# Whole-batch mixer sums in four column groups, more crossbar transposes and two-chunk exps in a fused attention and mixer kernel

## The chip, the cores and the metric

The kernel runs on one core of one Trainium2 chip. A core has five engines with queues of their own: TensorE (PE, matmuls; PEld is its weight load), VectorE (DVE), ScalarE (ACT), GpSimd (POOL) and SyncE (SP, which here only issues DMAs). Matmul results go to PSUM, eight banks of 128 partitions by 512 fp32. The metric is the device time of one execution in microseconds. The kernel before takes 286.63 us (median of 8 runs, 285.79 to 287.54).

## What is computed

Block-sparse attention over 4 batches, 8 heads, 768 positions and 64 channels a head, followed by a mixer. Blocks are 32 positions; the allowed blocks are the band, the first and last block, and three drawn blocks for each block of queries.

```python
scores = np.matmul(q, k.transpose(0, 1, 3, 2)) / np.sqrt(D)
scores = np.where(mask, scores, -1000000000.0)
attn = np.exp(scores - np.max(scores, axis=-1, keepdims=True))
attn = attn / (np.sum(attn, axis=-1, keepdims=True) + 1e-09)
x = np.matmul(attn, v)                  # (4, 8, 768, 64), then to (4, 768, 512)
h = x.transpose(0, 2, 1) @ U @ V        # U (768, 32), V (32, 768)
u = x + h.transpose(0, 2, 1)
out = u + np.maximum(u @ w_ch1, 0.0) @ w_ch2    # 512 -> 2048 -> 512
```

## The kernel before, in words

**Pairs and chunks.** Two heads make a pair; pair i belongs to batch i // 4, so there are 16 pairs. Keys are cut into six chunks g of 128. Scores are kept transposed: keys on partitions, 768 queries along the row. For each pair q, k and v are loaded in fp32 by SP (load_qk, load_v, two buffers each), cast to fp16 by POOL (cast, L132), and queries and keys are turned so that channels lie on partitions.

**Batch 0 and the later batches differ.** In batch 0 the mask is part of the contraction: qres and kres hold 64 channels of one head and 24 rows of a block bias. Each score step (S, L662) is two matmuls of 384 columns into two banks and one exp over one chunk of 768 on ACT (e). In the later batches the scores of both heads run as two row groups of 64 partitions (half_quad, L681, called by Q for both heads and by H for one); each head's exp covers two chunks (1536), and DVE multiplies the result by a 0/1 mask tile (p, L707). That mask tile is made in batch 0 (K and k). Exps land in est, 16 chunk slots handed out in twos (take_est).

**Turning.** Pairs 1 to 5 are turned on PE (turn_qk, R, six transposes for q and six for k) and copied by DVE (t). From pair 6 on, front (L371) does it by two DMA transposes through the crossbar, issued on SP; they are called in loads (L714), which also issues the loads of pair i + 2 and starts the weight loads: w1 (four 512 KB casts issued by POOL) behind the casts of pairs 2 and 3, w2 behind those of pairs 5 and 6. In later batches loads is called behind a pair's mixer sums.

**Values and mixer.** A value step multiplies a chunk of est with v and a column of ones (L398; A for one chunk, V for all six chunks of a head), and DVE divides (v: a reciprocal and two multiplications, into xh in fp16 and xf in fp32). The mixer runs pair by pair. M (mix, L482) is six matmuls of U's chunk, padded with zeros to 128 columns, with xh; m copies the 128x128 result to a16. D (add, L510) multiplies by V, and d adds the result to xh (into u16) and to xf. The second d of a pair also has SP issue the DMA transpose of u16 into uT (L528). Pairs 2 and 3 of batch 0 instead form uT on PE (X, Y, copy y), with E and g for xf; the very last pair is turned on PE (T, L551, copy x).

**Channel layers.** U (w1, L569) is four matmuls of 384 columns, one for each uT of the batch, followed by a relu on ACT (a) or DVE (b). In the first six such steps, P does three of the four matmuls and C the last. W (w2, L593) is four of the 16 matmuls of one output tile; behind the last of them DVE adds xf (f) and SP sends the tile out. L is half a tile at the very end.

**The order** is written out by hand in PLAN: a word in capitals issues a PE step (its digit is the first PSUM bank), a small letter issues the oldest result of its kind on DVE or ACT. PE, DVE, ACT and SP run exactly in this order; POOL's order is left to the framework. The head of the order is, with the first exps, casts and value steps:

```python
PLAN = """
S0 S3 e Z7 e z S0 S5 e Z2 e A7 z S3 A A e S0 S5 e A R2 e S3 t R1 e A A t S5 v e S3 S1 e K6
...
"""
```

The start (L238 to L326) brings the first head of pair 0 in: one cast on DVE and one on ACT, then the keys' first half is turned before the queries.

Of the kernel before, what the change touches and what calls it, by code (L numbers as in the profile page):

```python
# [2 lines left out]

# [14 lines left out]
P = 128  # L18
# [3 lines left out]
def kernel(  # L22
# [109 lines left out]
    def cast(i, dst, ld):  # L132

        if i < NPE:
            return nc.gpsimd.tensor_copy(out=dst, in_=ld)
        for h in range(2):
            for ts in (slice(0, T // 2), slice(T // 2, T)):
                last = nc.gpsimd.tensor_copy(out=dst[:, h, ts], in_=ld[:, h, ts])  # L138
        return last
# [25 lines left out]
    NPE = HP + 2  # L165
# [64 lines left out]
    with tc.manual_schedule(  # L230
# [71 lines left out]
        first_cast(0, 0, nc.vector.tensor_copy)  # L302
        first_cast(0, 1, nc.scalar.copy)
        first_turn(1, 0)
        first_row(1, 0, nc.scalar.copy)
        mask_half(0)
        for c in range(2):
            first_turn(0, c)
            first_row(0, c, nc.scalar.copy)
        mask_row(0, 0, nc.vector.tensor_copy)  # L310
        first_turn(1, 1)
# [68 lines left out]
    slots_of = {}  # L380

    def take_est(i, h, j):

        n = free_est.pop(0)
        for u in range(2):
            slots_of[i, h, 2 * j + u] = n + u
        return n

    def drop_est(i, h, g):
        n = slots_of.pop((i, h, g))  # L390
        if g % 2:
            free_est.append(n - 1)
# [14 lines left out]
    class Batch:  # L407
        def __init__(self):
            self.xf = xpool.tile([P, T, HD], FP32, tag="xf", name="xf", bufs=2)
            self.a16 = misc.tile([P, HD], FP16, tag="a16", name="a16", bufs=2)  # L410
            self.uT = [
                upool.tile([P, S], FP16, tag=f"uT{cc}", name=f"uT{cc}")
                for cc in range(NCC)
            ]
# [6 lines left out]
    S0 S3 e Z7 e z S0 S5 e Z2 e A7 z S3 A A e S0 S5 e A R2 e S3 t R1 e A A t S5 v e S3 S1 e K6  # L421
    A0 e A k K5 S3 k A e S6 S1 e K5 A e A k A S3 v K6 R7 e k S1 t e S3 S5 e R0 e S1 t A7 A e S3
    A A e S5 K0 K2 e A k A k S3 v A0 A e S1 A S5 e A K7 e S3 k K1 R2 e k A S5 t R7 e S3 t A S1 e
    v M6 e K5 S3 m k A7 A e S1 A A e S3 D0 A e S5 d R2 e S3 t A S0 e v M6 e D2 m S3 d A5 A e S0
    K7 A e S3 k A K6 e S0 k A A e S3 v R2 e S6 t S0 e S3 e A5 A e A D7 A K6 d S1 k D0 A e S3 d
    M7 e S1 m X6 A e S3 v Y A7 e S0 y E2 A e S3 g X5 Y e E6 A y A g A A Q v R6 e e t M7 X6 m Y p
    H y R7 e p H t U6 e p H b U7 e p H b P6 p e E2 V7 g p C Q v a V6 e e U7 v p P0 a M1 C P2 m p
    a C U6 a D7 Q a d D6 e e d U7 b U6 p U0 b U7 p a E6 Q a g U7 e e U6 b P7 b p X2 C V0 a p V4
    v P5 v Y P7 y C C M0 a a W6 m D7 Q d W e e D7 W d p W U7 f p Q a U7 e e W6 b U7 p U0 b W p a
    Q W e e W p U2 f V7 a p Q v V6 e e U7 v p U0 a U2 b U6 p a M7 a Q m D7 e e W6 d W p D7 W d p  # L430
    Q W e e W7 f p U0 V6 b p V1 v U2 v U0 a U4 a M5 a U6 m D0 U1 a d D6 W a d Q U6 e e W b W p
    W6 f p Q W e e U7 W p a W p Q f U7 e e W6 b U7 p W b p Q W e e W p U0 f V7 a p Q v V6 e e U7
    v p U0 a M1 a U6 m p U4 a D3 U1 a d D7 U6 a d Q b U7 e e U6 b U7 b p U1 a V6 p a V0 v U7 v
    U4 a M3 a U7 m U6 b D4 U2 a d U7 a D6 Q a d U7 e e W6 b U7 p W a p Q U7 e e W b W p U7 f p Q
    a U7 e e W6 b U7 p U0 b U1 p b V7 a Q v W e e V7 p U0 v W a p Q M7 e e W m W7 f p D0 D6 W d
    d p W Q W e e W6 f p W V7 p V1 v U4 v U7 a M0 a U2 m D1 W a d D5 W d W7 f Q W e e W p W W6 f
# [402 lines left out]
```

## Time and profile before

| what | value |
|---|---|
| median of 8 runs | 286.63 us |
| the profiled execution's own time | 286.92 us |
| its span on the core | 284.9 us |
| granted clock | 1.00 |
| PE, DVE, ACT, POOL busy | 277.2, 197.0, 179.1, 69.8 us |
| first exp of a score, first two-head score set | 7.38, 44.34 us |
| DVE busy in 44.3 to 64.0 us | 19.10 of 19.70 us |

Busy time of PE is modelled and includes the overlap of pipelined matmuls, so PE's pace is read from the chain of work that ended last, where pieces follow each other without overlap. The chain's pieces are "start, length, what, how many instructions". The lists in order of time give start, length, engine, line, operation, names and, in brackets, the idle time before and what ended it. ACT's two-chunk exp takes 1449 ns, the one-chunk exp 814 ns, but they overlap a little when they follow each other.

### The profile page before, as it was taken

The numbers are of one execution on the slowest core, as the hardware profiler recorded it, in microseconds if no ns is written. First come the engines' busy times: TensorE is split into PE (matmuls) and PEld (weight loads), VectorE is DVE, ScalarE is ACT, GpSimd is POOL, SyncE is SP. The second block draws the span as 40 slices with busy tenths as digits, with TensorE's granted clock in tenths as the row PEclk, the third lists the DMA queues.
The fourth block names the chain that finished last, engine by engine and source line by source line (L and its number), as shares of the span: only waits on it lengthen the run. The fifth ranks groups of instructions, "written<-read, shape, count | busy, mean of one in ns | idle before, by whom it ended". The sixth has DMA issues, their size and how long they took to land.

```text
span 284.9 us, 6730 instructions
## 1 busy us (share of the span) xinstructions
PE 277.2 (97%) x2770; PEld 163.5 (57%) x2770; DVE 197.0 (69%) x360; ACT 179.1 (63%) x213; POOL 69.8 (24%) x160
## 2 busy tenths in 40 slices
PE   7879999999999999999999999999999999999995
PEld 3557775657456654567556564565745565555553
DVE  5777989998768966788687885666866888231121
ACT  4979998885668466675776627777588730424200
POOL 5376127703151053401351033500310000000000
PEclk9999999999999999999999999999999999999999
DMA  5799999978370588108460499303741103001012
GB/s 175 232 317 245 230 213 222 182 122 202 63 236 28 90 242 243 62 19 223 101 211 2 98 224 216 134 17 60 225 86 39 39 37 86 18 0 40 37 55 92
DMA packets 46466, 36.78 MB, mean 129 GB/s; under 512 B 28036, under 2 KB 42948, under 8 KB 46436
## 3 DMA queue, kind: packets, MB, share of 16 engines
q1 hardware_dynamic: 43280, 31.80, 41.2%
q0 software_dynamic: 2688, 4.19, 8.3%
q8 instruction: 21, 0.34, 0.5%
q10 hardware_dynamic: 468, 0.36, 0.4%
q14 instruction: 9, 0.07, 0.1%
HBM read 27.66 MB, written 6.29 MB: 119 GB/s over the span
## 4 chain that ended last, share of the span: by engine, by line
PE 87%; DVE 6%; DMA 2%; POOL 2%; issue 1%; ACT 1%; SPq 1%; DVEq 0%; POOLq 0%; ACTq 0%
PE ps L569 29%; PE ps L593 28%; PE ps L398 11%; PE ps L692 9%; PE ps L669 3%; DMA kld<-in_k_dram 2%; PE ps L482 2%; PE ps L516 2%; PE ps L613 1%; PE ps L644 1%; DVE xh L463 1%; ACT est L678 1%; DVE est L707 1%; DVE u L523 1%; DVE xf L463 1%
## 5 line engine op out<-in xcount | busy, mean ns | idle before, releaser
L701 ACT ACTIVATE est<-ps 128x1536 f16<-128x1536 f32 x72 | 100.4, 1449 | 31.3 <-PE ps L692 31.3
L569 PE MATMUL ps<-uT,w1t 128*128 128x384 f16 x512 | 95.6, 326 | 0.4 <-DVE xf L526 0.2
L593 PE MATMUL ps<-w2t,tT 128*128 128x512 f16 x368 | 88.8, 379 | 0.0
L707 DVE TENSOR_TENSOR est<-est,mask 128x1536 f16<-128x1536 f16 x72 | 69.0, 960 | 13.4 <-ACT est L701 13.2
L581 ACT ACTIVATE tT<-ps 128x384 f16<-128x384 f32 x87 | 42.2, 493 | 54.0 <-PE ps L569 52.5
L569 PEld LDWEIGHTS <-w1t 128*128 128x128 f16 x512 | 47.4, 98 | 36.9 <-issue 6.6
L593 PEld LDWEIGHTS <-tT 128*128 128x128 f16 x368 | 34.4, 98 | 36.5 <-issue 2.9
L398 PEld LDWEIGHTS <-est 128*128 128x128 f16 x1152 | 40.7, 97 | 7.0 <-issue 1.2
L583 DVE TENSOR_SCALAR tT<-ps 128x384 f16<-128x384 f32 x41 | 22.8, 555 | 30.8 <-PE ps L569 30.3
L138 POOL CAST stqld<-qld 128x192 f16<-128x192 f32 x40 | 16.3, 450 | 112.0 <-DMA qld<-in_q_dram 98.5
L398 PE MATMUL ps<-vt,est 128*128 128x65 f16 x1152 | 43.3, 193 | 0.1
L678 ACT ACTIVATE est<-ps 128x768 f16<-128x768 f32 x48 | 34.8, 814 | 2.4 <-PE ps L669 2.3
L692 PE MATMUL ps<-qpl,kpl 64*128 64x512 f16 (+1 forms) x288 | 31.3, 325 | 0.0
L669 PE MATMUL ps<-qres,kres 128*128 128x384 f16 x96 | 22.2, 324 | 0.9 <-DVE kres L654 0.5
L601 DVE TENSOR_TENSOR of<-xf,ps 128x512 f32<-128x512 f32 x23 | 15.8, 685 | 9.8 <-PE ps L593 9.6
L692 PEld LDWEIGHTS <-kpl 64*128 64x128 f16 x288 | 11.7, 94 | 15.4 <-issue 9.5
L523 DVE TENSOR_TENSOR u<-xh,ps 128x384 f16<-128x384 f16 x28 | 15.4, 552 | 6.9 <-PE ps L516 6.1
L463 DVE TENSOR_TENSOR xh<-ps,rcp 128x384 f16<-128x384 f32 x32 | 17.8, 558 | 1.1
L463 DVE TENSOR_TENSOR xf<-ps,rcp 128x384 f32<-128x384 f32 x32 | 17.5, 547 | 0.0
L138 POOL CAST stkld<-kld 128x192 f16<-128x192 f32 x40 | 15.5, 428 | 1.3 <-DMA kld<-in_k_dram 0.6
L138 POOL CAST vt<-vld 128x192 f16<-128x192 f32 x40 | 15.2, 420 | 1.7 <-PE ps L692 1.4
L526 DVE TENSOR_TENSOR xf<-xf,ps 128x384 f32<-128x384 f32 x28 | 15.3, 548 | 0.0
(81 smaller groups left out, 143.0 us busy)
## 6 DMA issues: line engine op xcount, KB each, us to landing
vld<-in_v_dram SPq DMA_DIRECT2D x16, 384.0 KB, 4.6
out_dram<-of SPq DMA_DIRECT2D x23, 256.0 KB, 2.1
qld<-in_q_dram SPq DMA_DIRECT2D x15, 384.0 KB, 4.4
kld<-in_k_dram SPq DMA_DIRECT2D x15, 384.0 KB, 6.8
w1t<-in_moe_w_ch_dram POOLq DMA_DIRECT2D x4, 512.0 KB, 10.6
w2t<-in_moe_w_ch_dram POOLq DMA_DIRECT2D x4, 512.0 KB, 6.9
qld<-in_q_dram SPq DMA_DIRECT2D x2, 192.0 KB, 2.5
uT<-u SPq DMA_TRANSPOSE x13, 2.8
```

Source lines behind the costliest of these rows:

```text
L138: last = nc.gpsimd.tensor_copy(out=dst[:, h, ts], in_=ld[:, h, ts])
L398: nc.tensor.matmul(pav[:, sc, :], est[:, n, sc * P : (sc + 1) * P], vts[b % 2][:, 2 * hp + h, g, 0 : D + 1], start=(g == 0 and sc == 0), s ...
L463: self.last = nc.vector.tensor_tensor(out=dst, in0=pav[:, :, 0:D], in1=rcp[:, :, None].broadcast_to([P, T, D]), op=ALU.mult,)
L569: nc.tensor.matmul(pt, w1t[:, cc, jj * P : (jj + 1) * P], bts[b].uT[cc][:, c * HS : (c + 1) * HS], start=(cc == 0), stop=(cc == NCC - 1), ...
L581: nc.scalar.activation(out=dst, in_=pt, func=AF.Relu)
L583: nc.vector.tensor_scalar_max(out=dst, in0=pt, scalar1=0.0)
L593: nc.tensor.matmul(po, tts[b, c, jj][:, s * P : (s + 1) * P], w2t[:, jj, :], start=(jj == 0), stop=(jj == NJJ - 1),)
L669: nc.tensor.matmul(ps[:, c], kT[:, h, g * P : (g + 1) * P], qT[:, h, c * HS : (c + 1) * HS], start=True, stop=True,)
L678: lambda: nc.scalar.activation(out=dst, in_=ps, func=AF.Exp, scale=0.125),
L692: nc.tensor.matmul(units[h][:, u * S + lo : u * S + hi], kT[drows[h], g * P : (g + 1) * P], qT[drows[h], lo:hi], start=True, stop=True, sk ...
L701: nc.scalar.activation(out=both[h], in_=units[h].rearrange("p (g n) -> p g n", g=2), func=AF.Exp, scale=0.125,)
L707: lambda: nc.vector.tensor_mul(out=both[h], in0=both[h], in1=mask[:, 2 * j : 2 * j + 2, :]),
```

## The change

- **Whole-batch mixer sum.** In batches 1 to 3 the four M steps become one, mix_all. It keeps only U's 32 real columns as weights and writes four groups of 32 partitions of one bank: group c takes some of the six position chunks, so the four groups together hold U's sum in four parts. V is copied by DMA into all four groups of 32 rows (at pair 6), so that D adds the parts up. The sum comes behind the batch's last division, and all eight D of the batch behind it.
- **In place.** D's result goes back into xh (six buffers instead of three); u16 is gone.
- **Crossbar.** Pair 2 is handled like pairs 0 and 1 (D and the DMA transpose instead of X, Y, E), and so is the last pair (T is gone). Pairs 4 and 5 are turned by front, at the beginning of pairs 2 and 4, instead of R.
- **Two-chunk exps.** B does chunks 0 and 1, or 3 and 4, of a head in batch 0 into three banks with one exp of 1536. Ten of these replace twenty S. The est slots of a head are taken as (0,1), (2,5), (3,4).
- **Start.** Both first casts are on DVE; the queries are turned and copied before the keys.
- **Loads.** In the later batches loads is called behind a pair's second division. All of w1 starts behind the casts of pair 4; w2 starts when pair 2's second d is done (hold: four one-element copies on POOL that read xh and write into w2t).
- **Order.** PLAN is a new order of 867 words instead of 921.

```diff
-        first_cast(0, 0, nc.vector.tensor_copy)
-        first_cast(0, 1, nc.scalar.copy)
-        first_turn(1, 0)
-        first_row(1, 0, nc.scalar.copy)
-        mask_half(0)
+        for n in range(2):
+            first_cast(0, n, nc.vector.tensor_copy)
         for c in range(2):
             first_turn(0, c)
             first_row(0, c, nc.scalar.copy)
+        mask_half(0)
         mask_row(0, 0, nc.vector.tensor_copy)
+        first_turn(1, 0)
+        first_row(1, 0, nc.scalar.copy)
         first_turn(1, 1)
...
     PLAN = """
-    S0 S3 e Z7 e z S0 S5 e Z2 e A7 z S3 A A e S0 S5 e A R2 e S3 t R1 e A A t S5 v e S3 S1 e K6
...
+    B3 e S6 B0 e Z5 e S3 z Z7 e A6 z B0 A A e R7 S3 t A A e R5 B0 t K7 S3 e k K5 e A k A7 v A B0
+    K5 A e S3 k A A e K5 A k v B0 K6 S3 e k R5 e A7 A t M6 S1 m K0 e S5 k A S3 e S1 e R0 e A A t
+    S5 A S3 e v e B0 D6 A5 e A d A K7 A S3 k A K6 e A k B0 v S3 e e B5 A2 K0 e A R1 k A S3 t A
...
         def divide(self, h, pav):
...
+            if h and self.i >= HP:
+                loads(self.i + 1)
...
             def sums():
-                nc.vector.tensor_add(
-                    out=self.u16[:, ts, :], in0=self.xh[:, ts, :], in1=pu
-                )
+                nc.vector.tensor_add(out=xh, in0=xh, in1=pu)
                 nc.vector.tensor_add(out=xf, in0=xf, in1=pu)
-                if c == 1 and self.i < NPAIR - 1:
+                if c == 1:
                     nc.sync.dma_start_transpose(
...
-                    if self.i >= HP:
-                        loads(self.i + 1)
+                    if self.i == XP - 1:
+                        hold(self.xh)
...
+    def mix_all(b, n):
+
+        bt = bts[b]
+        pa = bank(n, [P, HD], FP32)
+        tiles = [[(c, hp) for hp in range(HP)] for c in range(4)]
+        for c in range(4):
+            tiles[c] += [(4 + c // 2, 2 * (c % 2) + u) for u in range(2)]
+        for m in range(HP + 2):
+            for c in range(4):
+                sc, hp = tiles[c][m]
                 nc.tensor.matmul(
+                    pa[c * R : (c + 1) * R, hp * P : (hp + 1) * P],
+                    Ut[:, sc, 0:R], bt.xh[hp][:, sc, :],
+                    start=(m == 0), stop=(m >= HP), skip_group_check=True,
+                )
+        then("m", lambda: nc.vector.tensor_copy(out=bt.a16, in_=pa))
...
+    def two_scores(i, h, g, n):
+        ps = PS[:, n : n + 3, :].rearrange("p b n -> p (b n)")
+        qT, kT = augs[i]
+        s = take_est(i, h, g, g + 1)
+        for u, lo, hi in SPANS:
+            nc.tensor.matmul(
+                ps[:, u * S + lo : u * S + hi],
+                kT[:, h, (g + u) * P : (g + u + 1) * P],
+                qT[:, h, lo:hi],
+                start=True, stop=True, skip_group_check=True,
+            )
...
     def loads(i):
         behind = ExitStack()
-        if NPE <= i + 1 < NPAIR:
+        if HP + 1 < i + 1 < NPAIR:
             behind.enter_context(tc.issue_after(front(i + 1).ins))
...
-            with tc.issue_after(last.ins):
-                if i == 0:
-                    load_w1((0, 1))
-                elif i == 1:
-                    load_w1((2, 3))
-                elif i == 3:
-                    load_w2((0, 4))
-                elif i == 4:
-                    load_w2((8, 12))
+            if i == 2:
+                with tc.issue_after(last.ins):
+                    load_w1(range(NCC))
+
+    def hold(behind):
+
+        for j in range(0, NJJ, 4):
+            nc.gpsimd.tensor_copy(out=w2t[0:1, j, 0:1], in_=behind[0:1, 0, 0:1])
+        load_w2(range(0, NJJ, 4))
...
-        if i <= HP:
-            loads(i)
+        if i == 2:
+            front(HP)
+        elif i == HP:
+            front(HP + 1)
+        elif i == HP + 2:
+            for c in range(1, 4):
+                nc.sync.dma_start(out=Vt[c * R : (c + 1) * R], in_=Vt[0:R])
+        for m in {0: (0,), 1: (1, 2), 3: (3,), 4: (4,)}.get(i, ()):
+            loads(m)
```

## The prediction

> **What bounds the kernel now.** I read the page's busy shares, then the slices, then ACT's list in order of time, then the chain that ended last, and at the end the DMA issues of SP.
>
> ```profile
> PE 277.2 (97%) x2770; PEld 163.5 (57%) x2770; DVE 197.0 (69%) x360; ACT 179.1 (63%) x213; POOL 69.8 (24%) x160
> ...
> DVE  5777989998768966788687885666866888231121
> ACT  4979998885668466675776627777588730424200
> ...
> PE 87%; DVE 6%; DMA 2%; POOL 2%; issue 1%; ACT 1%; SPq 1%; DVEq 0%; POOLq 0%; ACTq 0%
> ```
>
> PE looks full, yet the slices show ACT at nine tenths only up to 45 us, and DVE nearly full between 35 and 64. So there are two stages. The first is seen in ACT's own list:
>
> ```profile
> 7.38 8.11 ACT L678 ACTIVATE est<-ps 128x768 f16<-128x768 f32 x11 [0.57 <-PE ps L669]
> 15.70 2.95 ACT L678 ACTIVATE est<-ps 128x768 f16<-128x768 f32 x4 [0.20 <-PE ps L669]
> 20.21 23.79 ACT L678 ACTIVATE est<-ps 128x768 f16<-128x768 f32 x33 [1.57 <-PE ps L669]
> 45.20 8.28 ACT L701 ACTIVATE est<-ps 128x1536 f16<-128x1536 f32 x6 [1.20 <-PE ps L692]
> ```
>
> Thirty-three exps of batch 0 follow each other without a gap: the first two-head score set (Q) can only start at 44.34, when the last exp has freed its banks. From there to 281.81 the chain is PE almost without a break, and its pieces give PE's true pace:
>
> ```profile
> 112.07 0.76 PE ps L692 x8
> 112.83 0.76 PE ps L569 x4
> 113.58 0.86 PE ps L593 x4
> 114.44 0.65 PE ps L569 x4
> ...
> 119.20 1.09 PE ps L398 x36
> ...
> 166.66 0.34 PE ps L482 x6
> ```
>
> A w1 step is 0.65, a w2 step 0.86, six value products 0.18 (30 ns each), six 128-column products 0.33 (55 ns each), a Q 0.76. The first piece after a Q takes 0.11 more than elsewhere (0.76 against 0.65 here). Adding the whole old order at these paces gives 262.7 us of PE work; the first score began at 6.86 and PE ended at 281.81, so PE lost only 12.2 us: some 5.7 before the first Q, 3.7 as 34 Q's at 0.11, the rest mostly between 46 and 64.
>
> **The change, stage 1 (start to first Q, bound by ACT).**
> Start: both first casts on DVE (0.36 each there; ACT's took 0.51), queries first. ACT copies the two query halves while the keys arrive, then the first key half; by the rows' durations (key cast done at 4.80, its turn by 5.5, its copy 0.47) the first matmul can start near 6.3 instead of 6.86. It is now four matmuls (0.65) instead of two (0.32), so the first exp starts about 7.2 instead of 7.38: -0.2.
> ACT work: one-chunk exps run every 0.718 ((23.79-0.81)/32), two-chunk ones every 1.366 ((8.28-1.45)/5). Before 48 x 0.718 = 34.5; after 28 x 0.718 + 10 x 1.366 = 33.8: -0.7.
> ACT's waits before: 44.00 - 7.38 - 34.5 = 2.1, of which 1.57 ends at 20.21. There PE waits at the turn of pair 2's queries for their cast:
>
> ```profile
> 18.47 0.82 POOL L135 CAST stqld<-qld 128x768 f16<-128x768 f32 x1
> ```
>
> In the new order that turn stands behind 18 chunks, not 15 (about 2 us of exps later), so this wait goes; what is late next is the key cast (done at 20.06), also covered.
> A new wait comes: five of the ten two-chunk steps are B0 with only S3 between them and the preceding B0. Refilling three banks takes 0.65, plus 0.05 from exp to PE and 0.2 from PE to the next exp, against 0.64 left of the one exp of S3 that covers it: 0.27 each, +1.35.
> So the last exp ends near 7.2 + 33.8 + 1.35 = 42.4 and the first Q starts near 42.75 instead of 44.34: **-1.6**. PE has some 31 us of work before that Q and starts at 6.3, so it keeps 5 us of slack, which also covers the moved D steps, masks and turns; pair 4's turn (0.66) and pair 2's X and Y (0.65) go from here, worth nothing while ACT sets the end. Bounds: 0 (double refill waits, the cast still in the way) and -2.9 (no waits).
>
> **Stage 2 (first Q to the end, bound by PE).**
> Removed here: turning pair 5 (2 x 0.33 = 0.66), the last turn (L551, 0.33), and twelve mixer sums (12 x 0.33 = 3.96). Added: three whole-batch sums of 24 matmuls of 128x32 weights and 128 columns. No row shows column tiles. Nearest rows: the Q does two row tiles side by side (1.30 of streaming in 0.76), the value products set a pace of 30 ns for a pair of load and matmul. Lower bound: all four side by side, 0.33 + 0.11 for the switch = 0.44. Upper: one after the other, 24 x 0.055 + 0.11 = 1.43. I take the 30 ns pace, 0.73 + 0.11 = 0.84, as the shortest instruction pace seen. So -0.66 - 0.33 - 3.96 + 2.52 = **-2.4**; ends -3.6 and -0.7.
> [...]
> DVE: between the first Q and the third after it (44.34 to 63.58, 19.2 us) the old order gives it 18.3 us: 10 masks at 0.87, 3 divisions at 1.17, 2 D steps at 0.95, 8 copies, relus or single adds at 0.47, 2 narrow copies at 0.22. Pair 4's sums and pair 5's two copies leave this stretch: 15.7. Its first nine us stay bound by six exps (8.28); from the first to the third Q after it (53.96 to 63.58) PE had 8.6 + 0.2 of work in 9.6, so I take off **-0.5**; ends 0 and -0.8.
> ACT gets closer to PE: over the first eight Q's it has 34.2 us of work against 37.3 of PE (before 34.3 against 41.9), and the 0.32 to 0.43 that it idles ahead of a Q's exps make it about equal. I add **+0.4**; ends 0 and +1.5.
> The adds: a batch's eight (7.7 us of DVE) now come in one burst, in stretches where DVE is 0.7 to 0.85 busy. Behind them wait the transposes of uT (2.8 to landing), behind these w1 of that batch. PE work between the last add and the first w1 step that reads it is about 9, 7 and 8 us for batches 1 to 3 (its Q, w1, w2 and value steps at the paces above); add, issue and landing need about 5 to 6 with the burst's lag. So nothing is charged; if the cover were gone, up to 5 us a batch. Four crossbar fronts and two uT transposes more cost SP 1.2 each; between 21.9 and 34.5 SP only waits. The Vt copies (3 issues), hold's four tiny copies on POOL (0.1 each) and three 512-column a16 copies instead of twelve of 0.29 are hidden. w2 starts near 42 as now; its first use is after 70. w1 starts near 27 rather than 20 to 25; at 9 to 13 us each in parallel it lands near 42; the first w1 step stood 4.6 behind the first Q (48.92), so it is needed near 47.
>
> Sum: -1.6 - 2.4 - 0.5 + 0.4 = -4.1. The profiled run had 286.92 (span 284.9 and 2.0 around it), so 282.8; it lies 0.29 above the median, so **282.5**.
>
> **Rivals.**
> (a) More: column tiles fully side by side (-1.2) and the refill waits mostly covered (-1.0): 280.3. For it: two row tiles do overlap. Against: no row is below 30 ns a pair.
> (b) Less: column tiles in series (+1.8) and refill waits doubled (+1.3): 285.6. This is the change not doing what it says.
> (c) Slower: the chain of loads. SP now sends pair 4's transposes ahead of pair 5's load, pair 5's transposes ahead of pair 6's load, and so on; each transpose waits for POOL's casts, and w1's four transfers now run beside pair 5's load. By rows (casts 0.83, later 2 to 2.7; issue 1.22; load 4.4 to 7) pair 6 is ready near 62. Its Q, the fourth after the first, is due near 65 (42.75, then 9.6 to the next as before, then 4.5, 4.1 and 4.1 of PE pieces). Pair 4's keys took 9.3 from issue to cast under w1's traffic. If the loads of pairs 4, 5 and 6 take 2.5, 4 and 4 longer, the Q is 7.5 late and the time 290.0. It decides once the three delays sum to over 7.1 (3 of slack and the 4.1 gained). For it: DMA at full share from 24 to 60 us. Against: this share falls where w1 is moved out.
> (d) Slower: weight loads of column tiles are not hidden: 24 x (0.098 + 0.055) + 0.11 = 3.8 a batch, +8.8, 291.3. It decides from 2.2 us a batch. Against: 98 ns loads are hidden at a 30 ns pace in the value products.
>
> **How the numbers follow.** Forecast 0.48 (own range 281.0 to 284.0), (a) 0.20, (b) 0.15, (c) 0.12, (d) 0.05. About 0.2% (0.6 us) is what a measurement of this kernel tells from no change. Forecast, (a) and most of (b) are faster: 0.81; the rim of (b) towards (c) gives 0.04 the same; the rest, 0.15, slower. The range from 279.8 to 286.6 leaves out (c), (d) and the edge of (a).
>
> **What would show it.** First exp near 7.2; ten 1.4 us exps with 0.2 to 0.3 idle ahead of about half; no wait at 20; first Q near 42.7; whole-batch sums of 0.8 us each in the chain; no PE wait ahead of the first w1 step of a batch; DVE with gaps from 50 to 60. Wrong if PE waits for uT, w1t or qpl/kpl near 47 to 75, or if a whole-batch sum takes over 2 us.

## The result and the profile after

The changed kernel takes 293.24 us (median of 11 runs, 289.26 to 301.93) against 286.59 us for the kernel before on the same chips (32 runs, 285.30 to 288.09): a ratio of 1.0197 (95% interval 1.0170 to 1.0223). The forecast was 282.5, so the change made slower what it was forecast to make faster. The times of kernels with this loss scatter: medians and ranges here are of all runs, ratios leave out the runs more than 1.5% above a kernel's fastest. The profiled execution took 291.91 us with a span of 290.1.

From the page of the changed kernel: busy time, the granted TensorE clock in 40 slices of the span, and the shares of the chain that ended last.

```profile
PE 277.3 (96%) x2732; PEld 160.2 (55%) x2732; DVE 195.2 (67%) x347; ACT 177.2 (61%) x202; POOL 80.7 (28%) x164
...
PEclk9999999579999999999999999999999999999999
...
PE 88%; DVE 4%; ACT 3%; DMA 3%; issue 1%; ACTq 0%; DVEq 0%
```

PE's share still looks like a full engine. The one odd thing is the clock: 5 and 7 tenths in the eighth and ninth slices, 51 to 65 us. That is where the chain has to be read. Its pieces (start, length, what, how many instructions):

```profile
43.02 0.80 PE ps L731 x8
...
43.86 1.46 ACT est L740
...
45.34 0.96 DVE est L746
46.30 0.66 DVE uT L521 x2
46.96 5.17 DMA uT<-xh
...
52.18 0.80 PE ps L589 x2
52.98 1.39 PE ps L731 x4
54.37 1.39 PE ps L589 x4
55.76 1.39 PE ps L731 x4
57.15 1.07 PE ps L589 x3
...
60.85 1.12 PE ps L731 x6
```

The first two-head set (Q) starts at 43.02, near the forecast 42.75. Then the chain passes to a DMA: the crossbar transpose of pair 2's uT, issued at 46.96 and landed 5.2 us later. The w1 steps and the next Q stand behind it. Most of the standing still, though, is for an earlier one, as PE's own list of the first w1 step shows: it waited 3.45 us for pair 0's uT, issued at 35.03, and then 0.2 for each of the other two.

```profile
50.96 0.32 PE L589 MATMUL ps<-uT,w1t 128*128 128x384 f16 x1 [3.45 <-DMA uT<-xh]
```

Behind these waits the pieces of PE take about twice their time: 1.39 for a w1 step that takes 0.65 elsewhere. The same 16 us by windows of 4 us (columns: stretch, length, busy us and instructions of PE, PEld, DVE, ACT, POOL, then granted clock, DMA share, GB/s):

```profile
44.00:48.00 4.00, 3.02 (x22) 1.42 (x21) 3.51 (x7) 4.00 (x4) 1.24 (x2) 1.00 0.47 114
48.00:52.00 4.00, 0.80 (x2) 0.23 (x3) 1.59 (x2) 1.34 (x1) 4.00 (x8) 0.92 1.19 167
52.00:56.00 4.00, 3.82 (x11) 1.09 (x11) 1.62 (x3) 1.45 (x1) 1.70 (x3) 0.50 1.05 136
56.00:60.00 4.00, 4.00 (x36) 2.54 (x35) 2.64 (x4) 1.94 (x2) 0.00 (x0) 0.50 1.20 216
```

PE is busy for 0.80 of the four us from 48 to 52, and the clock is 0.50 for the eight us behind that. From the first Q to the second it was 9.6 us before (44.34 to 53.96) and is 17.8 now (43.02 to 60.85). By the prediction's paces the work in between is 7.9 and 7.6, so 1.7 was lost there before and 10.2 is lost now: 8.5 us more. The list of PE's waits (waiting line, what it waits for, us in total, times, longest) gives 3.9 of them:

```profile
PE ps L589 <- DMA uT<-xh: 3.9, 3, 3.5
```

The rest, 4.6, is the half clock: by windows of 0.2 us it lasts 10.24 us, from 51.2 to 61.4, and all but the last half us of it lies ahead of the second Q. The longest wait, of 3.5 us, is followed by 0.50 here, but the first experiment below has the same half clock behind waits of 0.4 us at most. The clock stays at 0.50 from 52 to 60 although PE is busy for 7.82 of these eight us.

Now SP's list in order of time, where the late transposes are issued ("SPq" is SP's queue; start, time until the issue was through):

```profile
24.43 1.75 SPq L374 DMA_TRANSPOSE qpl<-stqld  x1
26.23 1.26 SPq L374 DMA_TRANSPOSE kpl<-stkld  x1
27.54 0.72 SPq L148 DMA_DIRECT2D qld<-in_q_dram  x1
...
35.03 13.58 SPq L544 DMA_TRANSPOSE uT<-xh  x3
48.70 2.11 SPq L374 DMA_TRANSPOSE qpl<-stqld  x1
```

The prediction charged SP 1.2 us for each of these transposes. The three uT issues take 13.58 us together (9.27, 2.46 and 1.65 one by one). By DVE's rows the sums that they read were done at 35.0, 39.5 and 41.3, but the second and third went out only at 44.41 and 46.96, behind the first. Two lines of other views say how late the data was: POOL's list (pair 5's queries, whose load was issued at 27.54, are cast at 44.13 after 15.68 idle) and the uT tile between 30 and 62 us, where two of the three landings are listed, pair 0's of 15.8 and pair 1's of 7.1:

```profile
44.13 0.83 POOL L137 CAST stqld<-qld 128x768 f16<-128x768 f32 x1 [15.68 <-DMA qld<-in_q_dram]
```

```profile
DMA to landing us min/median/max: 7.1/11.4/15.8
```

What the DMA engines did meanwhile is in the DMA view of a stretch (queue, packets, MB, share of 16 engines). q0 is POOL's queue, which carries only w1 here; q1 is SP's. First 32 to 36 us, then 36 to 40:

```profile
q0 software_dynamic: 130, 0.49, 109.1%
q1 hardware_dynamic: 131, 0.03, 61.8%
```

```profile
q0 software_dynamic: 155, 0.57, 82.9%
q1 hardware_dynamic: 171, 0.15, 26.0%
```

130 packets of one, 131 of the other. A packet of w1 has 3.8 KB (0.49 MB over 130), one of SP's at that time 0.23 KB: these are transposes. A pair's 128x768 fp16 are 196 KB, and from 74.5 to 79.5 us, with no weight transfer near, two such transposes are 1607 packets under 512 bytes, some 800 each. From 32 to 36 SP's queue moved one packet for each of w1's, some 33 per us; at that pace a single transpose of 800 would by an estimate take over 20 us, or until w1 is through. That isn't all: from 40 to 44 us the counts are 81 to 832, and from 49.5 to 50.5, inside PE's long wait, SP's queue moves 30 packets although POOL's has moved none since 47. The experiments had to show what the cause is.

### The profile page after: what moved, and what is told of

Same layout as the page of the kernel before. It is cut to its first block, busy times and chain, and to the rows that moved or that the text cites. A ratio compares the mean times of both kernels' runs of the same rounds, so it can differ in the third digit from the quotient of the medians.

```text
span 290.1 us, 6631 instructions
## 1 busy us (share of the span) xinstructions
PE 277.3 (96%) x2732; PEld 160.2 (55%) x2732; DVE 195.2 (67%) x347; ACT 177.2 (61%) x202; POOL 80.7 (28%) x164
## 4 chain that ended last, share of the span: by engine, by line
PE 88%; DVE 4%; ACT 3%; DMA 3%; issue 1%; ACTq 0%; DVEq 0%
PE ps L589 30%; PE ps L613 28%; PE ps L401 11%; PE ps L731 10%; PE ps L687 2%; PE ps L529 2%; DMA uT<-xh 2%; ACT est L714 2%; PE ps L706 2%; PE ps L633 1%; ACT est L696 1%; DMA id<-eye_const 1%; DVE est L746 1%; PE ps L664 1%; DVE mask L656 1%
## 5 line engine op out<-in xcount | busy, mean ns | idle before, releaser
L740 ACT ACTIVATE est<-ps 128x1536 f16<-128x1536 f32 x72 | 100.5, 1448 | 47.0 <-PE ps L731 44.8
L746 DVE TENSOR_TENSOR est<-est,mask 128x1536 f16<-128x1536 f16 x72 | 70.6, 991 | 13.6 <-ACT est L740 13.6
L589 PEld LDWEIGHTS <-w1t 128*128 128x128 f16 x512 | 48.3, 98 | 42.7 <-issue 11.2
L401 PEld LDWEIGHTS <-est 128*128 128x128 f16 x1152 | 41.9, 98 | 9.2 <-issue 2.9
L401 PE MATMUL ps<-vt,est 128*128 128x65 f16 x1152 | 45.1, 195 | 0.2
L140 POOL CAST stqld<-qld 128x192 f16<-128x192 f32 x40 | 19.2, 521 | 87.2 <-issue 47.5
L603 DVE TENSOR_SCALAR tT<-ps 128x384 f16<-128x384 f32 x41 | 22.7, 556 | 30.7 <-PE ps L589 30.2
L731 PE MATMUL ps<-qpl,kpl 64*128 64x512 f16 (+1 forms) x288 | 33.0, 334 | 0.3 <-ACT est L740 0.3
L621 DVE TENSOR_TENSOR of<-xf,ps 128x512 f32<-128x512 f32 x23 | 15.7, 683 | 18.6 <-PE ps L613 16.6
L696 ACT ACTIVATE est<-ps 128x768 f16<-128x768 f32 x28 | 21.1, 817 | 0.0
L140 POOL CAST stkld<-kld 128x192 f16<-128x192 f32 x40 | 19.0, 514 | 1.7 <-DMA kld<-in_k_dram 1.7
L477 DVE TENSOR_TENSOR xh<-ps,rcp 128x384 f16<-128x384 f32 x32 | 17.8, 558 | 1.4 <-DVE rcp L472 0.3
L140 POOL CAST vt<-vld 128x192 f16<-128x192 f32 x40 | 18.0, 488 | 0.5 <-DMA vld<-in_v_dram 0.5
L541 DVE TENSOR_TENSOR xh<-xh,ps 128x384 f16<-128x384 f16 x30 | 16.4, 547 | 2.0 <-PE ps L529 2.0
L714 ACT ACTIVATE est<-ps 128x1536 f16<-128x1536 f32 x10 | 14.6, 1456 | 2.2 <-PE ps L706 2.2
```

What stands on the lines that cost most here:

```text
L401: nc.tensor.matmul(pav[:, sc, :], est[:, n, sc * P : (sc + 1) * P], vts[b % 2][:, 2 * hp + h, g, 0 : D + 1], start=(g == 0 and sc == 0), s ...
L477: nc.vector.tensor_tensor(out=dst, in0=pav[:, :, 0:D], in1=rcp[:, :, None].broadcast_to([P, T, D]), op=ALU.mult,)
L589: nc.tensor.matmul(pt, w1t[:, cc, jj * P : (jj + 1) * P], bts[b].uT[cc][:, c * HS : (c + 1) * HS], start=(cc == 0), stop=(cc == NCC - 1), ...
L603: nc.vector.tensor_scalar_max(out=dst, in0=pt, scalar1=0.0)
L696: lambda: nc.scalar.activation(out=dst, in_=ps, func=AF.Exp, scale=0.125),
L714: lambda: nc.scalar.activation(out=est[:, s : s + 2, :], in_=ps.rearrange("p (g n) -> p g n", g=2), func=AF.Exp, scale=0.125,),
```

## The experiments

The expectations name theories by letters: T1, that w1's later start delays uT; T2, that SP's order does (pair 4's transposes and pair 5's load ahead of uT); T3, that three transposes are slow in themselves; then T4, that any transpose started beside one of POOL's weight transfers lands late, whichever it is, and T5, that only the sum of DMA work between 24 and 56 us counts; at the end A and B, which are explained there. Unless said otherwise, edits are to the changed kernel. Each ratio is to the kernel before, whose median lay between 286.3 and 286.8 beside every group.

**w1 early.** w1 starts behind the casts of pairs 2 and 3, as in the kernel before.

```diff
-            if i == 2:
+            if i < 2:
                 with tc.issue_after(last.ins):
-                    load_w1(range(NCC))
+                    load_w1((2 * i, 2 * i + 1))
```

> Edit: w1's four transfers start behind the casts of pairs 2 and 3 again, as in the kernel before; all else as in the changed kernel. Theory T1: the three uT transposes (issued from 35.0, the last landing at 52.1) are late because w1's four transfers (25.4 to 47) share the DMA engines with them. Then with w1 gone by about 38 they land before 47, PE does not stop at 47.5, the granted clock stays 1.0 and about 8.5 us go (3.5 of standing still, 5 of half clock): 283 to 284. Rival T2: they are late because front(4) and pair 5's load stand ahead of them on SP's queue. Then moving w1 makes pair 4's load slower, as before the change (keys cast at 29.4), front(4) and pair 5's load move back by 3 to 5 us, and PE still stops: 288 or more.

Measured: 290.59 us (290.31 to 291.48), ratio 1.0167 [1.0133, 1.0200]. Pair 4's transpose of the keys now met w1 and was issued only at 31.75, pair 5's loads at 37.8 to 39.1, and the uT transposes behind them from 39.77; the last landed 5.87 us after 44.91. PE's three waits for uT shrank to 0.9 us, but the half clock came as before. PE's wait list and two windows of this run:

```profile
PE ps L589 <- DMA uT<-xh: 0.9, 3, 0.4
```

```profile
52.00:56.00 4.00, 4.00 (x13) 1.24 (x12) 2.50 (x4) 1.56 (x2) 1.64 (x3) 0.50 0.93 182
56.00:60.00 4.00, 4.00 (x47) 3.07 (x47) 1.90 (x4) 1.83 (x2) 1.94 (x4) 0.50 1.15 266
```

It lasted 10.24 us again, from 50.2, and from the first Q to the second it was 14.8 us (44.64 to 59.42), 5.2 more than before the change. So the larger part of the loss doesn't need a long wait. What halves the clock isn't shown: a wait of 1.8 us in pe45_w1e below is followed by 0.50 and one of 1.7 in the kernel with w2 behind pair 5's transposes is not. In the nine profiles that have it the half clock lasts 6.83, 10.24, 13.65 or 20.48 us (the last two in w1_cut and ut_act below), which are two, three, four and six times 3.41. T1 alone falls: the delay moved along SP's queue. (In this profiled run all of this is some 1.6 us late by the clock, as the first exp came at 8.96.)

**Pair 5's loads first.** w1 stays late; pair 5's loads go ahead of pair 4's transposes.

```diff
         if i == 2:
+            loads(3)
             front(HP)
...
-        for m in {0: (0,), 1: (1, 2), 3: (3,), 4: (4,)}.get(i, ()):
+        for m in {0: (0,), 1: (1, 2), 4: (4,)}.get(i, ()):
```

> Edit: pair 5's load is issued ahead of front(4) on SP, near 22.5 instead of 27.5, so ahead of w1; w1 stays late. T2 (SP's order): pair 5's load no longer stands between w1 and the uT transposes, PE does not stop: 283 to 284. T1 (w1's traffic): w1 still runs from 25 to about 44 beside the transposes, with 1.2 MB less to compete with; the stop shrinks but stays, and the half clock with it: 287 to 291.

Measured: 288.70 us, in two groups. Five runs lie between 284.61 and 287.54, with a mean clock of 0.999 to 1.00; the ratio, 0.9999 [0.9964, 1.0033], is theirs. Five lie between 289.86 and 295.54, at 0.971 to 0.988. In the profiled run (289.86, of the second group) the transpose of pair 4's keys, issued at 25.81, landed 22.36 us later, and the first Q slipped to 48.2. In the first group the loss against the kernel before is gone, though T2 had 283 to 284; no profile is of this group. So SP's order matters, but T2 alone doesn't give a time: which transpose is hit changes with the order, and whether one is hit changes from run to run.

**Both of these.**

> Edit: w1 early as in the kernel before, and pair 5's load ahead of front(4). T1 and T2 both expect no stop: 283 to 284. If it still stops, three transposes in a row are slow by themselves (T3), and the time stays above 288.

Measured: 292.12 us (289.40 to 293.10), ratio 1.0236 [1.0197, 1.0274]: worse, against the expectations. uT landed after 3.6 to 5.1 and the first w1 step ran at 47.5. But w2, held until pair 2's sums are done, now started at 42.7, and pair 5's transposes met it. From this kernel's chain:

```profile
25.25 15.28 DMA qpl<-stqld
...
44.58 12.07 DMA kpl<-stkld
```

The first transpose lay beside w1, the second beside w2. uT itself came in time, as T1 and T2 both had it, but their 283 to 284 didn't come, as another transpose was hit; T3 falls since three uT transposes in a row took 3.6 to 5.1. This run gave T4.

**Dummy matmuls.** Fourteen 512-column matmuls whose results nobody reads (a new step G) stand ahead of the first w1 step, to see whether the clock stays up when PE works through the wait.

```diff
-    M7 X6 m Y X7 p Y y H y e p H U7 e p ...
+    M7 X6 m Y X7 p Y y H y e p H G7 U7 e p ...
...
+    def dummy(n):
+        for _ in range(14):
+            nc.tensor.matmul(
+                PS[:, n, 0:512], warm[:, 0:P], warm[:, 0:512], start=True, stop=True
+            )
```

> Edit: 14 matmuls of 512 columns of constants (3.0 us at full clock) into a free bank just ahead of the first w1 step, where PE stands still from 47.5 to 51.0; nothing reads them. They neither hasten the transposes nor delay PE while it waits anyway. If about 5 of the 8.5 us lost are the half clock that follows the standstill, the granted clock stays 1.0 and the time is 287 to 288. If the loss is all waiting and the clock is only its shadow, nothing changes: 292.

Measured: 291.61 us. Four runs from 286.73 to 288.31 are near the expected 287 to 288, and the ratio, 1.0035 [1.0006, 1.0064], is theirs; the other six took 291.06 to 299.52. In the profiled run (286.85, of the four) the clock stayed at 0.998, but uT was nearly in time there, and a transpose of pair 5 was late instead (issued at 45.31, 10.92 to landing). The share of the half clock is therefore not separated by this run; it rests on the windows shown above and on the run with w1 early, where the wait is nearly gone and the half clock is not.

**Pairs 4 and 5 turned on PE again,** as in the kernel before, so that only the uT transposes are left on the crossbar in this stretch. Three kernels: with w1 late (pe45), with w1 early (pe45_w1e), and with w1 early and w2 held until pair 2's uT has landed (pe45_w1e_w2), for which the last two lines of the diff stand.

```diff
-        if i == 2:
-            front(HP)
-        elif i == HP:
-            front(HP + 1)
-        elif i == HP + 2:
+        if i == HP + 2:
...
-        "R": ((turn_qk, i, n) for i, n in each(range(1, HP), (0, 1))),
+        "R": ((turn_qk, i, n) for i, n in each(range(1, HP + 2), (0, 1))),
...
-                        hold(self.xh)
+                        hold(self.bt.turned(self.hp)[:, None, :])
```

> Edit: pairs 4 and 5 turned on PE again (R and t, four words put back into the order; no front(4), front(5)); w1 stays late, w2 as in the changed kernel. Theory T4, formed from the four runs before: a crossbar transpose that is started while one of POOL's weight transfers (w1, w2) is in flight lands after 5 to 22 us instead of 2.8, whichever transpose it is. w1 is in flight from 25 to 38 or 45, the uT transposes start at 35 to 41, so they stay late and PE stops ahead of the first w1 step: 286 to 290. Rival T5: it is the sum of the DMA work between 24 and 56 us; with four transposes fewer, uT lands by 47: 283 to 285.

> Edit: as pe45, and w1 early as in the kernel before (in flight 20 to 38). T4: the uT transposes of pairs 0 and 1 come behind w1 and land in about 3 us; pair 2's starts as w2 does and may take 5 to 8, where 6 are free: 283 to 286. T5: 283 to 284.

> Edit: as pe45_w1e, and w2 starts only when pair 2's uT has landed (POOL's tiny copies read uT instead of xh). T4: no transpose of the first 50 us runs beside a weight transfer, PE does not stop, clock 1.0: 282.5 to 284, which is the first prediction plus 0.7 for pair 5's turn on PE. T5: the same. If it still lies above 286, the loss is elsewhere.

Measured: 292.43 (1.0188 [1.0147, 1.0229]), 291.56 (1.0160 [1.0133, 1.0186]) and 285.50 us (0.9973 [0.9951, 0.9995]). In the first two, pair 2's uT was issued at 43.45 and 44.55 beside w2, started 0.3 to 0.4 before, and landed after 10.23 and 9.38; PE waited 2.6 and 1.8 for it, with 0.50 behind. Both times lie above what T4 and T5 had: that a transpose beside w2 is late fits T4, but the 9.38 is more than the 5 to 8 that it had for pe45_w1e. With w2 held back the one uT landing listed between 30 and 62 us took 3.6, the clock stayed at 1.00, and the loss against the kernel before was gone, though not down to the expected 282.5 to 284. Moving w2's start from 44.25 to 47.13 is worth six us by the medians; up to 1.5 of it may be the start, as the first exp came at 9.09 and at 7.57 in the two profiled runs.

**w2 behind pair 5's transposes,** with w1 early, pair 5's loads first, and the crossbar kept.

```diff
-                    if self.i == XP - 1:
-                        hold(self.xh)
...
         elif i == HP:
             front(HP + 1)
+            hold(plain(HP + 1)[1][:, None, :])
```

> Edit: as the run with w1 early and pair 5's load ahead of front(4), with crossbar turning of pairs 4 and 5 kept, but w2 starts only when front(5) has landed. T4: front(4) still runs beside w1 and lands near 40 (needed at 43), uT and front(5) run beside nothing and land in about 3 us, so the stop at 52.5 for pair 5's keys goes: 283 to 286. T5: the DMA work is the same, only later, so PE still stops somewhere between 48 and 70: 288 or more.

Measured: 284.98 us (283.67 to 286.91), ratio 0.9950 [0.9920, 0.9979]. Against the 292.12 of "both" the DMA work is the same and only w2's start moved, by 6.6 us: T5 falls. The first exp is at 7.29 and 7.36 in the two profiled runs, so the start has no part in it. The collision that is left is with pair 6's transposes, the keys landing 11.91 after 55.59, and costs only a wait of 1.7 us up to 67.5, with the clock at 1.00 behind it.

**w2 behind pair 6's transposes** instead of pair 5's.

```diff
             behind.enter_context(tc.issue_after(front(i + 1).ins))
+            if i == HP + 1:
+                hold(HP + 2, (0, 4, 8, 12))
```

> Edit: as both_w2 (w1 early, pair 5's load ahead of front(4)), but w2 starts only when front(6), pair 6's transposes, has landed. In both_w2 front(6) was issued at 54.3 and 55.6 beside w2 (49 to 61) and its keys landed at 67.5, where PE stood waiting for about 2 us. T4: that wait goes, w2 runs from about 59 to 70 and is needed near 72: 282.5 to 284, unless w2 itself comes late (then 284 to 286). T5 (amount of DMA work): no change to 285.

Measured: 284.05 us (283.18 to 285.83), ratio 0.9911 [0.9878, 0.9944]: faster than both kernels. From this kernel's profile the uT tile between 30 and 50 us, and the windows from 44 to 62, which in the changed kernel held 13.65 busy at a clock of 0.72:

```profile
DMA to landing us min/median/max: 2.8/3.1/3.5
```

```profile
44.00:62.00 18.00, 17.29 (x197) 9.97 (x194) 15.78 (x29) 15.58 (x16) 8.75 (x20) 1.00 0.82 182
```

**w2 in two halves,** two transfers behind pair 5's transposes and two behind pair 6's:

```diff
+            hold(HP + 1, (0, 4))
...
+                hold(HP + 2, (8, 12))
```

> Edit: as w2_after6, but the first two of w2's four transfers start when front(5) has landed and the last two when front(6) has. T4: front(6) is issued near 54 when the first two are nearly in (49 to 56), so it lands in 3 to 5 us; no stop: 282.5 to 284. T5: 285.

Measured: 284.82 us (284.25 to 286.85), ratio 0.9947 [0.9927, 0.9968]; no better than w2 in one, and above the expected 282.5 to 284.

**The whole-batch sums one column group after another,** on top of the two halves, to price what their side-by-side order gives.

```diff
-        for m in range(HP + 2):
-            for c in range(4):
+        for c in range(4):
+            for m in range(HP + 2):
```

> Edit: as w2_split, with the two loops of mix_all exchanged, so that six matmuls in a row go to one column group before the next group starts. If the changed kernel's 0.45 us for a whole-batch sum comes from four groups running side by side, the sum now takes 24 x 0.055 + 0.11 = 1.4 and the time is 2.5 to 3 us above w2_split. If 24 narrow matmuls are simply issued at 15 to 25 ns each, nothing changes.

Measured: 286.38 us (285.87 to 287.44), 1.56 us above the two halves. PE's list around the first such sum, in the kernel with interleaved groups and then in this one (where the next piece starts tells more than the modelled duration):

```profile
95.76 0.52 PE L566 MATMUL ps<-xh,Ut 128*32 128x128 f16 x24
96.21 1.90 PE L611 MATMUL ps<-w2t,tT 128*128 128x512 f16 x8
```

```profile
97.07 0.89 PE L566 MATMUL ps<-xh,Ut 128*32 128x128 f16 x24
97.89 1.47 PE L611 MATMUL ps<-w2t,tT 128*128 128x512 f16 x6
```

0.45 us against 0.82 for 24 matmuls: 19 and 34 ns each. Three sums make 1.1 of the measured 1.6. One group after another is still faster than the 55 ns per matmul of a 128-column product, so the expectation was too high.

**The kernel before with all of w1 behind pair 4's casts,** that is, its old order with w1 as late as in the changed kernel.

```diff
-                if i == 0:
-                    load_w1((0, 1))
-                elif i == 1:
-                    load_w1((2, 3))
+                if i == 2:
+                    load_w1(range(NCC))
```

> Edit to the kernel before, alone: all of w1 starts behind the casts of pair 4 instead of those of pairs 2 and 3. T4: the two uT transposes of pairs 0 and 1, issued at 34.5 and 40.9, now run beside w1 and land 3 to 15 us late; they are needed at 48.9, so the old kernel too gets a stop and a half clock: 288 to 294. T5: the old kernel's DMA work is unchanged and w1 lands near 43: 286 to 287.5.

Measured: 286.82 us (285.89 to 287.47), ratio 1.0012 [0.9993, 1.0030]. T4 had this slower. The DMA view tells why it is not, for 36 to 40 and for 40 to 44 us:

```profile
q0 software_dynamic: 196, 0.72, 97.4%
q1 hardware_dynamic: 75, 0.02, 2.5%
```

```profile
q1 hardware_dynamic: 1176, 0.85, 109.6%
q0 software_dynamic: 27, 0.07, 8.2%
```

The uT transpose issued at 34.97 moved 75 packets before 40, all of them after 39, while w1 moved 146 from 36 to 39: here the two queues don't take turns. The rest came as w1 ended, so it landed at least five us after its issue, late by T4's rule. But it was pair 0's, and the first w1 step comes at 49.3; the next transpose was issued at 41.36, when w1 was through. The kernel before has two such transposes ahead of the first w1 step, the changed one five, and pair 5's loads between them. A landing is listed only where somebody waited for it, so none is listed for these two.

Four more kernels were to tell what makes such a transpose late: that the two queues move packets in turn and SP's jobs go in order (A), or any weight transfer beside it (B).

**w1 in small packets:** the same bytes by columns, 1 KB of fp16 per row instead of 4.

```diff
-                out=w1t[:, cc, :], in_=moe_w_ch1[cc * P : (cc + 1) * P, :]
+                out=w1t[:, :, cc * HD : (cc + 1) * HD],
+                in_=moe_w_ch1[:, cc * HD : (cc + 1) * HD].rearrange(
+                    "(c p) d -> p c d", p=P
+                ),
```

> The changed kernel with w1's four 512 KB transfers taken by columns, 1 KB of fp16 per row instead of 4 KB; same bytes, start and engine. Theory A, formed from the packets per stretch of the runs so far: while POOL's queue and SP's queue both have work they move one packet each in turn, and SP's jobs go strictly in order, so the transposes of pair 4, the loads of pair 5 and the three uT transposes form one line whose pace is set by the weight's packets (in the changed kernel 130 to 153 of POOL's against 131 to 171 of SP's in 4 us between 32 and 40). With packets a quarter as large SP's queue should move 80 to 150 packets per us beside w1 instead of 30 to 47: pair 5's queries are cast before 41 instead of at 44.13, uT's transposes land after 3 to 10 us instead of 7.1 to 15.8, and PE waits less than 2 us for them instead of 3.9. w2 then starts earlier, near 45, and may meet pair 5's transposes as in the experiment that did both; time 286 to 292. Theory B (any transpose beside a weight transfer is late, whatever the packets): uT lands after 7 to 16 as before, PE waits 3 to 4.5, time 291.5 to 294.

Measured: 294.82 us (293.65 to 300.18), ratio 1.0270 [1.0229, 1.0311], above what either theory had. The profiled run is the longest of the four, 300.18. From 40 to 42 us of it:

```profile
q0 software_dynamic: 221, 0.22, 64.4%
q1 hardware_dynamic: 221, 0.32, 51.0%
```

The packets still go one for one, now 110 per us of each, and pair 5's queries were cast at 38.86 instead of 44.13: A's rule, and its number for the loads. Its consequence for uT didn't come: uT landed after 11.8 to 13.0 and PE waited 6.9 us in this run, where A had 3 to 10 and under 2. w1 in small packets was under way as long as in large ones (the slowest of its transfers landed 19.6 after its issue, against 19.0 in the changed kernel), and SP's line had to pass through it all the same. But w2, in packets of 1 KB too (317 for 0.31 MB from 58 to 60 us) and released at 45.5, was under way beside the last uT, for which PE waited until 57.7, and beside pair 5's keys (16.27 to landing); so this run doesn't show what w1's small packets alone do to uT. The turns were shorter here, the time of w1 was not.

**uT's transposes issued by ScalarE** instead of SP, in batch 0, on a queue of their own.

```diff
-                    nc.sync.dma_start_transpose(
+                    (nc.scalar if self.i < XP else nc.sync).dma_start_transpose(
```

> The changed kernel with the three uT transposes of batch 0 issued by ScalarE on a queue of its own instead of SyncE's; w1 and w2 as in the changed kernel. Theory A (SP's jobs go in order, so uT's lateness is mostly the line of pair 4's transposes and pair 5's loads ahead of it): uT lands after 3 to 8 us instead of 7.1 to 15.8, PE doesn't wait for uT near 47, w2 starts near 44 and meets pair 5's transposes, which are late instead; time 286 to 292, with 1 to 3 us more in stage 1 because ScalarE spends its time on the issues. Theory B (a transpose beside a weight transfer is late on whichever queue): uT lands after 7 to 16, PE waits for it, time 292 to 297.

Measured: 309.46 us (302.24 to 311.92), outside both expectations. ScalarE's list:

```profile
54.56 1.30 ACTq L544 DMA_TRANSPOSE uT<-xh  x1
55.91 1.51 ACT L696 ACTIVATE est<-ps 128x768 f16<-128x768 f32 x2 [18.60 <-issue]
```

ScalarE did no exp for 18.6 us around its first transpose, which went out 2.9 us after SP had issued the last of pair 5's (51.63). This run says nothing on A and B, as no uT transpose was under way beside w1, and what held ScalarE isn't shown. One thing it does show: w1 was issued at 27.6 to 30.7 and pair 5's queries, requested at 29.39, were cast at 48.13, with no uT in SP's line. With only pair 4's two transposes and the loads in it, that line took over 18 us beside w1.

**Only w2 moved,** behind pair 6's transposes; w1 stays late and SP's order as in the changed kernel.

> The changed kernel with w2 started only when pair 6's transposes have landed, and nothing else: w1 stays late, and the uT transposes stay behind pair 5's loads. Theories A and B: the standstill near 47 to 51 is w1's work alone and stays, with the half clock behind it; 290.5 to 293.5. If instead w2, which the changed kernel starts at 50.7, has a part in the loss (its transfers beside pair 5's transposes), the time falls to 286 to 289.

Measured: 293.65 us (291.98 to 298.15), ratio 1.0242 [1.0186, 1.0299], as expected but for 0.15. PE waited 3.8 for uT (7.1 to 15.8 in the changed kernel, 6.2 to 15.7 here), and the clock was 0.50 behind it. So in the changed kernel itself w2 has no part in the loss; w1 and the line on SP's queue, with pair 4's transposes and pair 5's loads ahead of uT, are left, and no run takes one of these two away with nothing else coming late. w2 takes w1's place as soon as w1 is out of the way.

**The fastest version with w1 in small packets.**

> The fastest version so far (w1 early, pair 5's loads ahead of pair 4's transposes, w2 behind pair 6's transposes; 284.05) with w1 in 1 KB packets. Theory A: pair 4's transposes beside w1 land 2 to 6 us earlier than there; nothing waits for them that sets the end, so 283.3 to 284.6. Theory B: they land as late as there, 283.7 to 284.5.

Measured: 283.87 us (283.35 to 284.26), ratio 0.9900 [0.9878, 0.9922]: the same time as with large packets, as both theories had it. A's turns are seen again, here in a run without loss: from 28 to 34 us the two queues moved 661 packets each, against 281 and 277 with large packets. That pair 4's transposes land 2 to 6 us earlier, as A had it, isn't seen: their landings aren't listed, and their issues were through at 37.1 instead of 38.8, in an execution whose first exp was 1.8 earlier.

**What the runs settle.** In these runs the time goes where one of POOL's weight transfers is under way together with crossbar transposes that PE needs soon. With w1 early and w2 behind the transposes, five kernels run at 283.9 to 285.5, and two pairs of kernels differ in w2's start alone; the transposes under way beside a weight transfer whose landing is listed landed 6.2 (w2_only) to 22.4 us (pair 5's loads first) after their issue. The turn of one packet each is read from the counts (130 to 131, 221 to 221) and held when the packet size was changed; the 146 to none above don't show it. Open is a second part: in some stretches a transpose moved next to nothing for four us while a weight transfer ran (75 packets between 36 and 40 above), or for one us while none did (49.5 to 50.5 in the changed kernel), and with transposes the pairs of packets came at 33 per us where loads beside w1 reach 48 (w1 early, 26 to 28 us: 96 and 100 packets in 2 us). No run separates what holds them, nor what halves the clock.

## Why the prediction was wrong, step by step

- **First exp, refill waits, first Q: right.** Forecast 7.2, 0.27 each and 42.75; measured 7.27, 0.20 to 0.38 and 43.02, with the wait at 20 gone. Stage 1 gained 1.3 of the 1.6. Not in every execution: in five of the profiled runs, that of the version with w2 behind pair 6's transposes among them, the first exp came at 8.96 to 9.13 (in that version its four score matmuls took 1.48 us instead of 0.82); the cause wasn't tried. From ACT's list after:

```profile
7.27 1.45 ACT L714 ACTIVATE est<-ps 128x1536 f16<-128x1536 f32 x1 [0.92 <-PE ps L706]
8.62 0.80 ACT L696 ACTIVATE est<-ps 128x768 f16<-128x768 f32 x1
...
11.67 1.45 ACT L714 ACTIVATE est<-ps 128x1536 f16<-128x1536 f32 x1 [0.20 <-PE ps L706]
```

- **Stage 2 without the collision: right.** From the first Q to PE's end it was 237.5 us before (44.34 to 281.81) and is 234.6 in the version with w2 behind pair 6's transposes (44.77 to 279.33): -2.9, forecast -2.5. Within it, the whole-batch sum was mis-sized: 0.84 taken, 0.45 measured with 0.1 on the next piece. The lower bound, all four groups side by side, was the right one, and rival (a)'s reading of it; the 30 ns that the prediction took as the shortest pace is not the least here (19 ns measured). Three sums at 0.3 less each are 0.9 more than forecast, so the other terms of this stage gave about 0.5 less: that -2.9 is so near -2.5 is in part luck.
- **The step that failed: the transposes costed at nothing.** "the transposes of uT (2.8 to landing)" took their price from the only landings listed in the trace of before, those of the later batches with no weight transfer near. "Four crossbar fronts and two uT transposes more cost SP 1.2 each; between 21.9 and 34.5 SP only waits" counted the issue and not the packets, and "w1 starts near 27 ... lands near 42" was taken without what is in the same queues: one of w1's four transfers, all issued by 28.5, took 19.0. The waiting instruction was PE's first w1 step, and behind it stood the second Q and ACT's next exps: 8.5 us, of which 3.9 are waits for uT and the half clock, which no step had priced, is more than half.
- **Rival (c)** had slower loads as its mechanism and gave 290.0, near the result. It put the wait at pair 6's Q near 65; it came at uT at 47, and pair 5's loads, though POOL waited 15.7 for them, could set the end only as part of the line ahead of uT. The prediction's own list of what would make it wrong, PE waiting for uT near 47, is what happened.
- **Sum of the profiled runs.** Stage 1 -1.3, stage 2 +5.6 (8.5 lost, 2.9 gained), and +0.9 behind PE's last matmul (span minus PE's end 3.1 before, 4.0 after, and 4.0 in the version with w2 last too): span +5.2, from 284.9 to 290.1. The 0.9 at the end was not foreseen and its cause not tried. Of the 4.1 forecast, 2.5 (medians 286.59 and 284.05) arrive when the collision is taken out; in that version's profiled run (285.06) the first Q is at 44.77, 0.4 later than before, by the late start named above.

## What to carry to other kernels

A DMA's price from a quiet stretch didn't hold beside a bulk transfer on another queue here (2.8 us to landing in the quiet, 15.8 beside w1): count packets (some 800 a transpose), not bytes or issues, and what stands ahead in the same queue, before more transposes are put into a loading phase. Let a bulk transfer that is needed late start behind the small transfers that are needed soon; here moving w2's start was worth 7 us (292.12 against 284.98). And look at the granted clock behind late data: here the half clock cost 4.6 us and the waits 3.9, and in one run it came with no wait over 0.4 us.

## What the runs showed of the hardware that was not expected

- In many stretches two DMA queues with work moved one packet for one: 130 and 131 in 4 us with 3.8 KB against 0.23 KB, 221 and 221 in 2 us with 1.0 against 1.45 KB. In others they didn't: 146 and none from 36 to 39 in the kernel before with late w1. A 128x768 fp16 transpose that landed in 2.8 us alone took 6.2 to 22.4 us beside a weight transfer, where its landing is listed.
- A standstill of 3.5 us, and in another run three waits of 0.9 us in all, was followed by 10.24 us at a clock of 0.50, though PE was 96 to 100% busy in eight of them. In other kernels it was 6.83, 13.65 (w1_cut) or 20.48 us (ut_act); 6.83, 10.24, 13.65 and 20.48 are two, three, four and six times 3.41.
- 24 matmuls with 128x32 weights and 128 columns in four column groups take 0.45 us when the groups alternate, 19 ns each, and 0.82 us group after group; the shortest pace of full-width products here is 30 ns.
